# A block-causal attention and a two-layer feed-forward network on one core: one scheduling block with the detailed timing model, TensorE in program order

## The chip, the cores and the metric

The kernel runs on one core of a Trainium2 chip. The time is the device time of one execution in microseconds. Before the change it was 1272.79 us, the median of three runs (1271.26 to 1273.68).

## The reference

All arrays are float32.

```
scores = scale * matmul(q, k^T)              # batch 8, heads 8, 576 tokens, head size 64
mask   = block_i >= block_j                  # blocks of 64 tokens: a causal mask by blocks
attn   = softmax(where(mask, scores, -1e9))
x      = (attn @ v), heads side by side      # 4608 x 512
h      = x @ w_in                            # 4608 x 2048
g      = h where h >= 1, 0 where h <= -1, else (h + 1)^2 / 4
out    = g @ w_out                           # 4608 x 512
```

## The kernel before

A float32 operand that must keep its precision is split into a rounded high part and the rest, so that products run as two or three faster matmuls. The two weight matrices are split by `convert` in 64 pieces of 128x256. A piece is a load on the SP queue, two multiplications on ScalarE (L165, L166), three operations on VectorE (L167, L170, L173), then GpSimd (L179), ScalarE (L181) and GpSimd (L183). The pieces of `w_out` are gathered in `ws` tiles and written back to DRAM as `wo_split`.

Attention goes through 32 pairs of heads, pair 0 to pair 31, four for each batch. A pair is a generator of eight steps: loads and splits of q and k (`split_q`, `split_k`), their transposes on TensorE (`turned`, L346, and `turned_last`, L365), scores (`product`, L391 and L394), maximum on VectorE (L414), exponential on ScalarE with its sum read out (L418), normalisation (L400, L401, L424), transposes of the result (`turn`, L461 or L463; from pair 4 on the result first goes through a transfer, `as_float32r`), splits of it (L454, L456) and the product with v (L500). The next pair's transposes of q and k belong to the steps of the pair before it: the first transposes of its k, `nxt.turned(False, 0)`, stand at the end of the step that computes `cur.scores(1, 1)`. In the first two batches (pairs 0 to 7) the product with v is done in plain float32.

The network works on chunks of 512 tokens and 16 slices of 128 hidden units, 144 in all. `ffn_in` accumulates twelve matmuls in the one bank `ph` (L646), then ScalarE (L655), VectorE (L656, L659), ScalarE (L660) and GpSimd (L661) make `gh` and `gl`; `ffn_out` adds twelve matmuls into four banks `po` (L670, L675). From step 36 of attention on (the middle of pair 4) one network step, an `ffn_in` or an `ffn_out`, is emitted after each step of attention. What is left follows after the last pair.

The tiles of scores and transposes share PSUM banks, `work_bank`: three of them once the network runs. So a tile waits until what was in its bank three tiles earlier has been read.

What sets the order: the program emits instructions in the order above. A scheduler then orders each engine's queue by priority, the emission order, and by the readiness that a timing model gives, and also hands out the buffers. On the chip every queue is worked off strictly in its order. Before the change this is one simple timing model for all queues, TensorE's among them.

Of the kernel before, what the change touches and what calls it, by code (L numbers as in the profile page):

```python
# [23 lines left out]
def block_attn_then_ffn(  # L24
# [59 lines left out]


    ident_f = ffn.tile([P, 512], F32, tag="t", name="ident_f")[:, :P]
    make_identity(nc, ident_f)
    ident_r = const.tile([P, P], F32R, tag="ident", name="ident_r")
    nc.vector.tensor_copy(ident_r, ident_f)
    ident = ident_r.bitcast(F32)  # L90

    xh = const.tile([P, NCC, RING], F32R, tag="xh", name="xh")
    xl = const.tile([P, NCC, RING], F32R, tag="xl", name="xl")
    wih = const.tile([P, NCC, DF], F32R, tag="wih", name="wih")
    wil = const.tile([P, NCC, DF], F32R, tag="wil", name="wil")
    wo_split = dram.tile([NFC, P, 2, DM], F32, tag="wo_split", name="wo_split")
# [3 lines left out]
    qa = const.tile([P, 2, QW], F32R, tag="qa", name="qa")  # L100
    qb = const.tile([P, 2, QW], F32R, tag="qb", name="qb")
    ka = const.tile([P, 2, S], F32R, tag="ka", name="ka")
    kb = const.tile([P, 2, S], F32R, tag="kb", name="kb")

    def last_blocks(t_):

        view = t_[:, :, SM : SM + BLK]
        if t_.shape[2] == S:
            return view
        part, (_, two), cols = view.ap  # L110
        return bass.AP(tensor=view.tensor, offset=view.offset, ap=[part, [QW + BLK, two], cols])


    mrow = att1.tile([NTL, 2, S], F32R, tag="pb0", name="mrow")


    pcs = [const.tile([P, 2, BLK], F32R, tag=f"pcs{i}", name=f"pcs{i}") for i in range(2)]
    vsr = [const.tile([P, NTL + 1, 2, D], F32R, tag=f"vsr{j}", name=f"vsr{j}") for j in range(2)]

    mtmp = ffn.tile([P, 512], F32, tag="t", name="mtmp")  # L120
    msel = ffn.tile([P, 512], F32, tag="t", name="msel")
    nc.vector.memset(mtmp, 0.0)
    nc.vector.memset(msel[:NTL], 0.0)
    nc.gpsimd.affine_select(
        out=msel[:NTL, : NTL * BLK].rearrange("p (t c) -> p t c", c=BLK),
        in_=msel[:NTL, : NTL * BLK].rearrange("p (t c) -> p t c", c=BLK),
        compare_op=ALU.not_equal, fill=1.0, base=0,
        pattern=[[-1, NTL], [0, BLK]], channel_multiplier=1,
    )
    sel = msel[:NTL, : NTL * BLK].rearrange("p (t c) -> p t c", c=BLK)  # L130
    for side in range(2):
        nc.vector.tensor_copy(mrow[:, side, :512], mtmp[:NTL, :512])
        nc.vector.tensor_copy(mrow[:, side, 512:S], mtmp[:NTL, : S - 512])
    rows = mrow[:, :, :SM].rearrange("p s (t c) -> p s t c", c=P)
    nc.vector.tensor_copy(rows[:, 0, :, :BLK], sel)
    nc.vector.tensor_scalar_mul(rows[:, 1, :, BLK:], sel, MASKED)
    for t_ in (qa, qb):
        nc.vector.tensor_copy(
            t_[:, :, SM:], mtmp[:, : 2 * (QW - SM)].rearrange("p (h c) -> p h c", h=2)
        )  # L140
    for t_ in pcs:
        nc.vector.tensor_copy(t_[BLK:], mtmp[BLK:, : 2 * BLK].rearrange("p (h c) -> p h c", h=2))
    for t_ in vsr:
        nc.vector.tensor_copy(
            t_[BLK:, NTL, :, :], mtmp[BLK:, : 2 * D].rearrange("p (h c) -> p h c", h=2)
        )
    for j in range(2):
        nc.sync.dma_start(qa[D:KA, j, :S].bitcast(F32), mrow[:, 0, :].bitcast(F32))
        nc.sync.dma_start(ka[D:KA, j, :].bitcast(F32), mrow[:, 1, :].bitcast(F32))


    def convert(n, source, hi, lo, done):

        if n < BORROW and n % 2:
            bits = ffn.tile([P, CW, 2], I32, tag="t", name="bits")
            work = ffn.tile([P, 2, CW], F32, tag="gl", name="work")
        else:
            bits = conv.tile([P, CW, 2], I32, tag="bits", name="bits")
            work = conv2.tile([P, 2, CW], F32, tag="work", name="work")
        nc.sync.dma_start(bits, source.bitcast(I32).rearrange("p (n t) -> p n t", t=2))  # L160
        top, mag = work[:, 0, :], work[:, 1, :].bitcast(U32)
        low = bits[:, :, 0]


        nc.scalar.mul(top, bits[:, :, 1].bitcast(F32), 2.0**-112)  # L165
        nc.scalar.mul(low, low.bitcast(U32), 2.0**-29)  # L166
        nc.vector.tensor_scalar(  # L167
            out=top, in0=top, scalar1=F32_TOP, scalar2=-F32_TOP, op0=ALU.min, op1=ALU.max
        )
        nc.vector.tensor_scalar(  # L170
            out=mag, in0=top.bitcast(U32), scalar1=3, scalar2=None, op0=ALU.logical_shift_left
        )
        nc.vector.scalar_tensor_tensor(  # L173
            out=mag, in0=top.bitcast(U32), scalar=0x80000000, in1=mag,
            op0=ALU.bitwise_and, op1=ALU.bitwise_or,
        )
        yield
        w32 = mag.bitcast(I32)
        nc.gpsimd.tensor_tensor(out=w32, in0=w32, in1=low, op=ALU.add)  # L179
        w32 = w32.bitcast(F32)  # L180
        nc.scalar.copy(hi(), w32)  # L181
        yield
        nc.gpsimd.tensor_tensor(out=lo(), in0=w32, in1=hi().bitcast(F32), op=ALU.subtract)  # L183
        if done:
            done()

    def weight_pieces():

        for f0 in range(0, DF, CW):
            fs = slice(f0, f0 + CW)  # L190
            for cc in range(NCC):
                yield (
                    w_in[cc * P : (cc + 1) * P, fs],
                    lambda cc=cc, fs=fs: wih[:, cc, fs], lambda cc=cc, fs=fs: wil[:, cc, fs], None,
                )
            for fc in range(f0 // P, (f0 + CW) // P):
                ws = {}

                def part(w, d0, ws=ws):
                    if not ws:  # L200
                        ws[0] = ffn.tile([P, 2, DM], F32R, tag="wo", name="ws")
                    return ws[0][:, w, d0 : d0 + CW]

                for d0 in range(0, DM, CW):
                    yield (
                        w_out[fc * P : (fc + 1) * P, d0 : d0 + CW],
                        lambda p_=part, d0=d0: p_(0, d0), lambda p_=part, d0=d0: p_(1, d0),
                        None if d0 + CW < DM else
                        lambda fc=fc, ws=ws: nc.sync.dma_start(wo_split[fc], ws[0].bitcast(F32)),
                    )  # L210

    def prepare_weights():

        live = []
        for n, piece in enumerate(weight_pieces()):
            live = [c for c in live + [convert(n, *piece)] if next(c, True) is None]
            yield
        for _ in range(LAG):
            live = [c for c in live if next(c, True) is None]
            yield  # L220
# [3 lines left out]
    spare = {"n": 0, "of": []}  # L224

    def as_float32r(src, plain):

        if plain:
            if not spare["of"]:
                spare["of"] = [t_[:, :NTL, :, :].rearrange("p t h d -> p (t h d)") for t_ in vsr]  # L230
                spare["of"].append(att1.tile([P, S], F32R, tag="x32", name="prs")[:, :TCH])
                spare["end"] = att1.tile([P, G0 + P], F32R, tag="pa11", name="pre")[:, :BLK]
            moved = [spare["of"][spare["n"] % 3]]
            spare["n"] += 1
            if src.shape[1] > TCH:
                moved.append(spare["end"])
            for i, dst in enumerate(moved):
                n = min(TCH, src.shape[1] - i * TCH)
                nc.sync.dma_start(dst[:, :n].bitcast(F32), src[:, i * TCH : i * TCH + n])
            return moved  # L240
        moved = []
        for c0 in range(0, src.shape[1], TCH):
            n = min(TCH, src.shape[1] - c0)
            pool, tag = ((conv, "bits"), (conv2, "work"))[c0 > 0]
            dst = pool.tile([P, TCH], F32R, tag=tag, name="prr")
            nc.sync.dma_start(dst[:, :n].bitcast(F32), src[:, c0 : c0 + n])
            moved.append(dst)
        return moved


    class Pair:


        GROUPS = (((0, 0), (1, P)), ((2, 0),), ((3, 0),))

        def __init__(self, b, hp):
            self.b, self.hp = b, hp

            self.plain = b < PLAIN
            self.first = b == 0 and hp == 0  # L260

# [467 lines left out]
    for _ in ffn_steps:  # L729
        pass  # L730
# [30 lines left out]
```

## Time and profile before

| | us |
|---|---|
| median of three runs | 1272.79 |
| profiled execution, its own time | 1272.09 |
| its span, first to last instruction | 1270.3 |
| TensorE busy (matmuls) | 1210.7 |
| VectorE busy | 856.4 |
| ScalarE busy | 701.3 |
| GpSimd busy | 456.3 |
| mean granted TensorE clock | 0.985 |

The span is cut into stretches in the prediction, because its stages have different limits: the first 266 us hold pairs 0 to 7 and all conversions, the rest is a steady alternation of attention and network steps and, from about 1083 us, the network alone. In a row of the profile, "<-" behind a duration in brackets names what ended the engine's wait before that instruction, with the length of the idle time ahead of it. PE is TensorE, PEld its weight loads, DVE VectorE, ACT ScalarE, POOL GpSimd, SP the queue that issues the transfers.

### The profile page before, as it was taken

Reading aid. Unit: us, or ns where it says so; the run is one execution under the profiler, and the core shown is the slowest. Engines: PE = TensorE matmul, PEld = TensorE weight load, DVE = VectorE, ACT = ScalarE, POOL = GpSimd, SP = SyncE. Lnnn points to the kernel's source line nnn. Section 1 sums busy time; section 2 is a strip of 40 time slices with the busy share of each in tenths; the row PEclk is TensorE's granted clock in tenths of the full one; section 3 lists DMA queues with packets and bytes.
Section 4 is the critical chain, followed back from the end, with each engine's and each line's share of the span. In section 5 each row is a group of like instructions: output and inputs, shape, how many; then the busy total and the mean of one; then the engine's idle time right before and its main releaser. Section 6 shows DMA issues by size and latency. Waiting matters only on the chain.

```text
span 1270.3 us, 20591 instructions
## 1 busy us (share of the span) xinstructions
PE 1210.7 (95%) x6496; PEld 1018.4 (80%) x6496; DVE 856.4 (67%) x2164; ACT 701.3 (55%) x1827; POOL 456.3 (36%) x454
## 2 busy tenths in 40 slices
PE   5879887899999999999999999999999999999998
PEld 4667666688888888888888888888888888888886
DVE  8998877857776777777777777777777676222222
ACT  5877656546565655566556656555565564222222
POOL 3555655523332333333333333333333332222222
PEclk9888989899999999999999999999999999999999
DMA  5656666655444545564455545454445443322432
GB/s 157 182 165 213 196 228 210 212 184 173 148 152 147 191 144 161 158 193 149 148 162 168 178 141 161 153 181 143 152 154 184 151 132 117 127 92 97 133 100 100
DMA packets 146093, 201.30 MB, mean 158 GB/s; under 512 B 63152, under 2 KB 93872, under 8 KB 145984
## 3 DMA queue, kind: packets, MB, share of 16 engines
q1 hardware_dynamic: 145984, 199.98, 50.4%
q8 instruction: 52, 0.85, 0.3%
q14 instruction: 57, 0.47, 0.1%
HBM read 120.59 MB, written 17.83 MB: 109 GB/s over the span
## 4 chain that ended last, share of the span: by engine, by line
PE 68%; DVE 8%; ACT 4%; issue 3%; DMA 3%; POOL 2%; SPq 0%; ACTq 0%; POOLq 0%; DVEq 0%
PE ph L646 26%; PE po L670 16%; PE po L675 8%; PE ps_av L500 7%; PE ps_t L461 3%; PE ps_s L394 3%; PE ps_s L391 3%; ACT pr L418 2%; PE ps_qk L346 2%; DMA prr<-pr 2%; DVE t L656 2%; DVE nm L414 1%; DVE t L659 1%; DVE pr L424 1%; POOL work L179 1%
## 5 line engine op out<-in xcount | busy, mean ns | idle before, releaser
L661 POOL TENSOR_TENSOR gl<-t,gh 128x512 fp32r<-128x512 f32 x144 | 186.9, 1298 | 604.7 <-ACT gh L660 301.8
L670 PE MATMUL po<-wo,gh 128*128 128x512 f32 x1152 | 296.9, 399 | 0.1
L656 DVE SCALAR_TENSOR_TENSOR t<-t 128x512 f32<-128x512 f32 x144 | 112.9, 784 | 200.2 <-ACT t L655 198.5
L646 PE MATMUL ph<-xh,wih 128*128 128x512 f32 x576 | 237.6, 413 | 2.7 <-DVE t L659 1.8
L670 PEld LDWEIGHTS po<-wo,gh 128*128 128x128 f32 x1152 | 207.7, 188 | 39.3 <-ACT gh L660 0.6
L646 PE MATMUL ph<-xl,wih 128*128 128x512 f32 x576 | 227.4, 395 | 0.9 <-DVE xl L536 0.9
L646 PE MATMUL ph<-xh,wil 128*128 128x512 f32 x576 | 227.4, 395 | 0.0
L655 ACT ACTIVATE t<-ph 128x512 f32<-128x512 f32 x144 | 86.1, 598 | 184.7 <-PE ph L646 184.7
L418 ACT ACTIVATE pr<-ps_s,nm 128x128 f32<-128x128 f32 (+3 forms) x256 | 134.4, 529 | 50.6 <-DVE nm L414 50.3
L414 DVE TENSOR_REDUCE nm<-ps_s 128x1 f32<-128x128 f32 (+3 forms) x256 | 123.6, 485 | 48.7 <-PE ps_s L394 47.4
L675 PE MATMUL po<-wo,gl 128*128 128x512 f32 x576 | 155.3, 391 | 0.0
L660 ACT CAST gh<-t 128x512 fp32r<-128x512 f32 x144 | 89.6, 622 | 102.1 <-DVE t L659 101.7
L391 PE MATMUL ps_s<-ka,qa 68*128 68x288 f32 (+4 forms) x384 | 122.5, 334 | 9.1 <-ACT kb L351 4.2
L646 PEld LDWEIGHTS ph<-xh,wil 128*128 128x128 f32 x576 | 109.1, 189 | 24.1
L675 PEld LDWEIGHTS po<-wo,gl 128*128 128x128 f32 x576 | 108.1, 188 | 23.3
L646 PEld LDWEIGHTS ph<-xh,wih 128*128 128x128 f32 x576 | 109.1, 189 | 21.7 <-DVE t L659 2.4
L646 PEld LDWEIGHTS ph<-xl,wih 128*128 128x128 f32 x576 | 109.6, 190 | 20.2 <-DVE xl L536 1.5
L394 PE MATMUL ps_s<-kb,qb 128*128 128x288 f32 (+4 forms) x384 | 121.4, 323 | 0.0
L454 ACT CAST pb<-ps_t 128x512 fp32r<-128x512 f32 (+1 forms) x120 | 65.5, 546 | 85.6 <-PE ps_t L461 83.8
L424 DVE TENSOR_SCALAR pr<-pr,sm 128x128 f32<-128x128 f32 (+3 forms) x256 | 104.8, 430 | 4.0
L336 POOL TENSOR_TENSOR vsr<-vn,vsr 64x64 fp32r<-64x64 f32 (+1 forms) x96 | 72.8, 768 | 88.6 <-ACT vsr L335 88.6
L456 DVE TENSOR_TENSOR pb<-ps_t,pb 128x512 fp32r<-128x512 f32 (+1 forms) x120 | 75.6, 630 | 40.4 <-ACT pb L454 39.9
(101 smaller groups left out, 1961.4 us busy)
## 6 DMA issues: line engine op xcount, KB each, us to landing
wo<-wo_split SPq DMA_DIRECT2D x144, 512.0 KB, 3.4
prr<-pr SPq DMA_DIRECT2D x96, 192.0 KB, 2.7
prr<-pr SPq DMA_DIRECT2D x72, 256.0 KB, 2.6
out_dram<-ob SPq DMA_DIRECT2D x36, 256.0 KB, 3.9
qn<-in_q_dram SPq DMA_DIRECT2D x32, 256.0 KB, 2.9
kn<-in_k_dram SPq DMA_DIRECT2D x32, 256.0 KB, 2.9
bits<-in_moe_w_in_dram SPq DMA_DIRECT2D x32, 256.0 KB, 3.6
bits<-in_moe_w_out_dram SPq DMA_DIRECT2D x32, 256.0 KB, 3.2
```

The source lines that it names most:

```text
L391: nc.tensor.matmul(ps, qa[:KA, j, c0 : c0 + P], ka[:KA, j, k0 : k0 + n], start=first, stop=False)
L394: nc.tensor.matmul(ps, qb[:, j, c0 : c0 + P], kb[:, j, k0 : k0 + n], start=False, stop=last)
L414: nc.vector.tensor_reduce(out=nm[:, i : i + 1], in_=ps[:, cs], axis=AX.X, op=ALU.max, negate=True)
L418: nc.scalar.activation(pr[:, cs], ps[:, cs], AF.Exp, bias=nm[:, i : i + 1], scale=1.0, accum_out=sm[:, i : i + 1],)
L424: nc.vector.tensor_scalar_mul(pr[:, cs], pr[:, cs], sm[:, i : i + 1])
L500: nc.tensor.matmul(ps[:, lo_col:], vt, x, start=first and i == 0 and m == 0, stop=last and i == len(parts) - 1 and m == len(mov) - 1,)
L646: nc.tensor.matmul(ph, w[:, cc, fs], x[:, cc, xs], start=(cc == 0 and i == 0), stop=(cc == NCC - 1 and i == 2),)
L656: nc.vector.scalar_tensor_tensor(out=t_, in0=t_, scalar=1.0, in1=t_, op0=ALU.min, op1=ALU.mult)
L660: nc.scalar.copy(gh, t_)
L661: nc.gpsimd.tensor_tensor(out=gl, in0=t_, in1=gh.bitcast(F32), op=ALU.subtract)
L670: nc.tensor.matmul(po[tt], gh[:, ts_], wo[:, w, :], start=(fc == 0 and w == 0), stop=False)
L675: nc.tensor.matmul(po[tt], gl[:, ts_], wo[:, 0, :], start=False, stop=fc == NFC - 1)
```

## The change

One line is added after the definition of `work_bank`, and everything that follows in the function is indented under it. So each line below it has a number higher by one in the changed program.

```diff
+    with tc.block(schedule_with_timeline_sim=True), tc.manual_schedule(engines={mybir.EngineType.PE}):
...
-    ident_f = ffn.tile([P, 512], F32, tag="t", name="ident_f")[:, :P]
-    make_identity(nc, ident_f)
+        ident_f = ffn.tile([P, 512], F32, tag="t", name="ident_f")[:, :P]
+        make_identity(nc, ident_f)
...
```

TensorE's queue is now the emission order, instruction by instruction. The queues of VectorE, ScalarE, GpSimd and SP are ordered with the second, more detailed timing model, and the buffers are handed out along with that. No instruction is added or removed. From pair 8 on the queues differ in a few places for each pair; in the first eight pairs they differ throughout.

**TensorE, pair 14, the step of `cur.scores(1, 1)`.** `prr` is the transferred result of the softmax, `ks` the split k of pair 15, `ph` the network's bank. Before:

```order
L394 MATMUL ps_s<-kb,qb 128x384
L461 MATMUL ps_t<-ident_r,prr 128x128 x4
L461 MATMUL ps_t<-ident_r,prr 64x128
L646 MATMUL ph<-xh,wih 128x512
L646 MATMUL ph<-xl,wih 128x512
L646 MATMUL ph<-xh,wil 128x512
...
L346 MATMUL ps_qk<-ident_r,ks 128x128 x4
L646 MATMUL ph<-xh,wih 128x512
```

Changed:

```order
L395 MATMUL ps_s<-kb,qb 128x384
L462 MATMUL ps_t<-ident_r,prr 128x128 x4
L462 MATMUL ps_t<-ident_r,prr 64x128
L347 MATMUL ps_qk<-ident_r,ks 128x128 x4
L647 MATMUL ph<-xh,wih 128x512
L647 MATMUL ph<-xl,wih 128x512
```

The four transposes of k stood behind six of the step's twelve `ph` matmuls and now stand ahead of all of them. The place recurs in each pair from 8 to 30.

**ScalarE, the same step.** `gh` is the network's rounded slice, `pr,sm` an exponential with its sum, `pb` and `pcs` rounded parts of the turned result, `kb` the copy of the turned k. Before:

```order
L660 CAST gh<-t 128x512
L418 ACTIVATE pr,sm<-ps_s,nm 128x128
L418 ACTIVATE pr,sm<-ps_s,nm 128x256
L454 CAST pb_5432<-ps_t 128x4x2x64
L418 ACTIVATE pr,sm<-ps_s,nm 128x384
L454 CAST pcs_107<-ps_t 64x128
L351 CAST kb<-ps_qk 128x512
```

Changed:

```order
L419 ACTIVATE pr,sm<-ps_s,nm 128x128
L419 ACTIVATE pr,sm<-ps_s,nm 128x256
L661 CAST gh<-t 128x512
L455 CAST pb_5435<-ps_t 128x4x2x64
L455 CAST pcs_110<-ps_t 64x128
L419 ACTIVATE pr,sm<-ps_s,nm 128x384
L352 CAST kb<-ps_qk 128x512
```

The two exponentials of `cur.scores(1, 0)` move ahead of the `gh` cast, and the small cast of `pcs` moves ahead of the exponential of `cur.scores(1, 1)`. On VectorE the two reductions of `cur.scores(1, 0)` likewise move ahead of the network's L656.

**VectorE, the start of the program.** `ident_r` is the identity for the transposes, `qs` and `ks` the split q and k, `work` a weight conversion, `qa` and `ka` the copies of turned q and k. Before:

```order
L311 SCALAR_TENSOR_TENSOR qs<-qn,qs 128x9x64
L320 CAST ks<-kn 128x8x64
L320 CAST ks<-kn 128x64
L321 TENSOR_TENSOR ks<-kn,ks 128x9x64
L89 CAST ident_r<-ident_f 128x128
L135 CAST mrow<-msel 4x4x64
L136 TENSOR_SCALAR mrow<-msel 4x4x64
L167 TENSOR_SCALAR work<-work 128x256
L170 TENSOR_SCALAR work<-work 128x256
L353 CAST qa<-ps_qk 64x512
L353 CAST ka<-ps_qk 64x512
```

Changed:

```order
L90 CAST ident_r<-ident_f 128x128
...
L312 SCALAR_TENSOR_TENSOR qs<-qn,qs 128x9x64
L136 CAST mrow<-msel 4x4x64
L137 TENSOR_SCALAR mrow<-msel 4x4x64
L321 CAST ks<-kn 128x64
L322 TENSOR_TENSOR ks<-kn,ks 128x9x64
L354 CAST qa<-ps_qk 64x512
L354 CAST ka<-ps_qk 64x512
L415 TENSOR_REDUCE nm<-ps_s 128x1 x3
```

The identity's cast moves ahead of the splits, and the first weight conversion moves behind the copies `qa` and `ka` and the first reductions. ScalarE's queue moves its share of that conversion (L165) behind the copies of the turned q and k in the same way. After that the conversions run ahead: VectorE's queue holds 33 of the 64 ahead of the first reduction of pair 4, where it held 25.

More of the change, by code (lines that the diff above doesn't have):

```diff
@@ L114, in block_attn_then_ffn @@
[L114 to L129, printed above, removed]
@@ L141, in block_attn_then_ffn @@
[L141 to L185, printed above, removed]
@@ L212, in prepare_weights @@
[L212 to L248, printed above, removed]
@@ L496, in weighted @@
-        def weighted(self, ps, j, parts, first=True, last=True):
-            for i, (kt, lo_col, mov) in enumerate(parts):
-                vt = self.vs[j][: (BLK if self.plain and kt == NTL else P), kt, :, :]
-                for m, x in enumerate(mov):
-                    nc.tensor.matmul(
-                        ps[:, lo_col:], vt, x,
-                        start=first and i == 0 and m == 0,
-                        stop=last and i == len(parts) - 1 and m == len(mov) - 1,
-                    )
@@ L689, in feed_forward @@
-    def feed_forward():
-        prev = None
-        for c in range(NCH):
-            for fc in range(NFC):
-                cur = (c, fc, *ffn_in(c, fc))
-                yield
-                if prev is not None:
-                    if prev[1] == 0:
-                        po = [ps_o.tile([P, DM], F32, tag="po", name="po") for _ in range(NTT)]
-                    ffn_out(po, *prev)
-                    yield
-                prev = cur
-        ffn_out(po, *prev)
-        yield
-    START = 8 * NPAIR + 4
@@ new lines, in ffn_in @@
+        def ffn_in(c, fc):
+            at = (c * TCH) % RING
+            ph = ps_h.tile([P, 512], F32, tag="ph", name="ph")
+            fs = slice(fc * P, (fc + 1) * P)
+            xs = slice(at, at + TCH)
+            for cc in range(NCC):
+                for i, (w, x) in enumerate(((wih, xh), (wih, xl), (wil, xh))):
+                    nc.tensor.matmul(
+                        ph, w[:, cc, fs], x[:, cc, xs],
+                        start=(cc == 0 and i == 0), stop=(cc == NCC - 1 and i == 2),
+                    )
+            t_ = ffn.tile([P, TCH], F32, tag="t", name="t")
+            gh = ffn.tile([P, TCH], F32R, tag="gh", name="gh")
+            gl = ffn.tile([P, TCH], F32R, tag="gl", name="gl")
+            nc.scalar.activation(t_, ph, AF.Relu, bias=0.5, scale=0.5)
+            nc.vector.scalar_tensor_tensor(
+                out=t_, in0=t_, scalar=1.0, in1=t_, op0=ALU.min, op1=ALU.mult
+            )
+            nc.vector.tensor_tensor(out=t_, in0=ph, in1=t_, op=ALU.max)
+            nc.scalar.copy(gh, t_)
+            nc.gpsimd.tensor_tensor(out=gl, in0=t_, in1=gh.bitcast(F32), op=ALU.subtract)
+            wo = ffn.tile([P, 2, DM], F32R, tag="wo", name="wo")
+            nc.sync.dma_start(wo.bitcast(F32), wo_split[fc])
+            return gh, gl, wo
@@ new lines, in ffn_out @@
+        def ffn_out(po, c, fc, gh, gl, wo):
+            for tt in range(NTT):
+                ts_ = slice(tt * P, (tt + 1) * P)
+                for w in range(2):
+                    nc.tensor.matmul(
+                        po[tt], gh[:, ts_], wo[:, w, :], start=(fc == 0 and w == 0), stop=False
+                    )
+            for tt in range(NTT):
+                ts_ = slice(tt * P, (tt + 1) * P)
+                nc.tensor.matmul(po[tt], gl[:, ts_], wo[:, 0, :], start=False, stop=fc == NFC - 1)
+            if fc < NFC - 1:
+                return
+            for tt in range(NTT):
+                ob = conv.tile([P, DM], F32, tag="bits", name="ob") if tt % 2 else conv2.tile(
+                    [P, DM], F32, tag="work", name="ob"
+                )
+                if tt % 2:
+                    nc.scalar.copy(ob, po[tt])
+                else:
+                    nc.vector.tensor_copy(ob, po[tt])
+                r0 = c * TCH + tt * P
+                nc.sync.dma_start(out[r0 : r0 + P, :], ob)
@@ new lines, in feed_forward @@
+        def feed_forward():
+            prev = None
+            for c in range(NCH):
+                for fc in range(NFC):
+                    cur = (c, fc, *ffn_in(c, fc))
+                    yield
+                    if prev is not None:
+                        if prev[1] == 0:
+                            po = [ps_o.tile([P, DM], F32, tag="po", name="po") for _ in range(NTT)]
+                        ffn_out(po, *prev)
+                        yield
+                    prev = cur
+            ffn_out(po, *prev)
+            yield
```

933 lines of the change are left out of this document (491 added, 442 removed).

## The prediction

> **What bounds the kernel now.** I read the page's span and busy shares first, then the busy time by stretches, then the waits, then the order of time at one place.
>
> ```profile
> span 1270.3 us, 20591 instructions
> PE 1210.7 (95%) x6496; PEld 1018.4 (80%) x6496; DVE 856.4 (67%) x2164; ACT 701.3 (55%) x1827; POOL 456.3 (36%) x454
> ```
> TensorE is busy for 95% of the span, so only about 60 us can be won anywhere. Where they lie is shown by stretches: up to the first scores, pairs 0 to 3, pairs 4 to 7, pairs 8 to 31 and the end. Pair 4 starts at 100.56 and pair 8 at 265.95, each with its first reduction of scores.
>
> ```profile
> 0.00:14.00 14.00, 3.81 (x23) 3.62 (x24) 9.12 (x29) 4.50 (x10) 2.52 (x10) 1.00 0.52 132
> 14.00:100.60 86.60, 70.65 (x366) 57.28 (x366) 79.83 (x246) 69.04 (x211) 46.67 (x57) 0.88 0.60 177
> 100.60:266.00 165.40, 144.66 (x713) 113.84 (x712) 129.46 (x323) 104.49 (x297) 91.59 (x109) 0.95 0.67 214
> 266.00:1083.00 817.00, 809.35 (x4602) 693.85 (x4601) 588.57 (x1498) 479.37 (x1240) 271.44 (x244) 1.00 0.51 157
> 1083.00:1271.00 188.00, 182.19 (x800) 149.82 (x798) 49.40 (x72) 43.87 (x73) 44.09 (x34) 1.00 0.32 107
> ...
> 477.00:510.65 33.65, 33.42 (x193) 28.71 (x193) 24.61 (x64) 19.83 (x51) 11.50 (x10) 1.00 0.48 152
> ```
> After the length come busy PE, PEld, DVE, ACT and POOL, then the granted clock. In pairs 0 to 3 VectorE is the bound: 79.83 of 86.60 us. In pairs 4 to 7 nothing is saturated: TensorE 144.66 of 165.40 us at a clock of 0.95, VectorE 129.46. From 266 us on TensorE works without a break (809.35 of 817.00), so there each microsecond in which its queue stands still is added to the end. The last row is one period of that stretch, 33.65 us for a pair.
>
> **The change, part by part.** 1. TensorE's queue in pairs 8 to 31. It was nearly the program's order already. Of the places that differ one recurs in each of pairs 8 to 30, 23 times: the four transposes of the next pair's k stood behind the first 6 (17 places) or 7 (6 places) of the twelve `ph` matmuls of that step, and now stand ahead of them. Here is that place in pair 14, TensorE first, then VectorE and ScalarE.
>
> ```profile
> 491.28 0.35 PE L391 MATMUL ps_s<-ka,qa 68*128 68x384 f32 x1
> 491.47 0.34 PE L394 MATMUL ps_s<-kb,qb 128*128 128x384 f32 x1
> 491.65 0.53 PE L461 MATMUL ps_t<-ident_r,prr 128*128 128x128 f32 x5
> 492.01 0.45 PE L646 MATMUL ph<-xh,wih 128*128 128x512 f32 x1
> 492.30 0.40 PE L646 MATMUL ph<-xl,wih 128*128 128x512 f32 x1
> ...
> 493.22 0.39 PE L646 MATMUL ph<-xh,wil 128*128 128x512 f32 x1
> 493.83 0.54 PE L346 MATMUL ps_qk<-ident_r,ks 128*128 128x128 f32 x4 [0.23 <-ACT pr L418]
> 494.21 0.46 PE L646 MATMUL ph<-xh,wih 128*128 128x512 f32 x1
> ```
> ```profile
> 491.22 0.60 DVE L400 TENSOR_SCALAR sm<-sm 128x2 f32<-128x2 f32 x1 [0.57 <-ACT pr L418]
> ...
> 492.52 0.55 DVE L414 TENSOR_REDUCE nm<-ps_s 128x1 f32<-128x384 f32 x1
> ```
> ```profile
> 492.15 0.59 ACT L454 CAST pb<-ps_t 128x512 fp32r<-128x512 f32 x1 [0.96 <-PE ps_t L461]
> 493.11 0.58 ACT L418 ACTIVATE pr<-ps_s,nm 128x384 f32<-128x384 f32 x1 [0.37 <-DVE nm L414]
> 493.59 0.19 ACT L418 ACTIVATION_READ_ACCUMULATOR pr<-ps_s,nm 128x1 f32 x1
> 493.68 0.25 ACT L454 CAST pcs<-ps_t 64x128 fp32r<-64x128 f32 x1
> ```
> The transposes write the bank that held this step's scores. They wait for reduction and exponential of them, released at 493.78, and start at 493.83. The chain is the same in the changed program; what goes is its cover, six matmuls from 492.01 to 493.45. The queue reaches the transposes at 492.01 and stands, and everything behind them stands too: the twelve `ph` matmuls, then all of `ffn_out`. The cover is 17 x 6 + 6 x 7 = 144 matmuls of 0.23 us (492.30 to 493.22 is four of them), 33.1 us. Two things come off. In the new queues the casts of `pb` and `pcs` stand ahead of the exponential and the reduction is earlier (the two reductions and exponentials of the step before move ahead of the `t` and `gh` work), so the exponential starts when the casts end, 492.74 plus about 0.23, near 492.97 in place of 493.11: 0.14 us, 3.2 us in 23 places. And the waits quoted below name 13 stops at these transposes, so in some 8 places TensorE came after the release, by up to one matmul, 0.2 us: 1.6 us. **Sum +28 us.** From below: the reduction cannot start before the scores end (491.81), and reduction, exponential and read-out take 0.55 + 0.58 + 0.10 with two hand-overs of 0.05, release near 493.1; TensorE then loses 1.1 - 0.38 = 0.7 us, 16 us in all. From above: no link shorter and the cast of `pcs` (0.25) on the chain, 33.1 + 5.8 = 39 us. I take 28, which is what the row at 492.15 gives.
>
> The other moves in these pairs are a few places on VectorE and ScalarE. Here and there a normalisation whose result is transferred before its turn comes later by a few short instructions of the q and k split. That costs nothing while the transfers have margin, and the waits show they have:
>
> ```profile
> PE ps_qk L346 <- ACT pr L418: 2.9, 13, 0.3
> PE ps_t L461 <- DMA prr<-pr: 1.6, 4, 0.6
> PE ps_t L461 <- ACT pr L418: 0.8, 2, 0.5
> ```
> These are all of TensorE's named waits from 266 to 1050 us: 5.3 us. It is also the most that this part could win.
>
> 2. The start.
>
> ```profile
> 7.57 0.56 PEld L346 LDWEIGHTS ps_qk<-ident_r,qs 128*128 128x128 f32 x4 [7.57 <-DVE ident_r L89]
> 10.26 0.43 ACT L165 ACTIVATE work<-bits 128x256 f32<-128x256 f32 x1 [8.25 <-DMA bits<-in_moe_w_in_dram]
> 10.72 0.29 DVE L167 TENSOR_SCALAR work<-work 128x256 f32<-128x256 f32 x1 [2.81 <-ACT work L165]
> 12.72 0.47 PE L391 MATMUL ps_s<-ka,qa 68*128 68x128 f32 x1 [2.62 <-DVE ka L353]
> ```
> A weight conversion stands ahead of the first `qb` and `qa` copies and holds both queues until its data land. Now the conversions stand behind, and the identity's cast ahead of the q and k splits. That wins the 2.81 us, and I take **-3 us** (bounds -5 and 0).
>
> 3. The conversions. Counting VectorE's rows ahead of the first reduction of pair 4, 25 of the 64 conversions stood there and now 33; ahead of pair 8 it is all 64 in both.
>
> ```profile
> L167 DVE TENSOR_SCALAR work<-work 128x256 f32<-128x256 f32 x24 | 11.3, 476 | 0.8 <-ACT work L165 0.8
> L173 DVE SCALAR_TENSOR_TENSOR work<-work 128x256 uint32<-128x256 uint32 x24 | 10.9, 453 | 0.1
> L170 DVE TENSOR_SCALAR work<-work 128x256 uint32<-128x256 uint32 x24 | 10.1, 424 | 0.1
> ```
> One costs 476 + 453 + 424 = 1353 ns, so 8 more on the saturated engine put pair 4 **+10.8 us** later (bounds +4, if they fit into the 6.8 us that VectorE is idle there, and +14). Pairs 4 to 7 get 8 fewer. Against that stands TensorE's fixed order there: some fifteen places where attention's matmuls stood behind `ph` or `po` matmuls now stand ahead of them. The first bounds are 0 and the 20.7 us that TensorE idles in these pairs, and since VectorE is only 78% busy I take -6. The second costs between 0 and 15 x 1.4 = 21 us by the steady place; many of those waits are there already, so I take +10. The twelve matmuls of the first `ffn_in`, which filled gaps of pairs 2 to 4, now run in pair 4: 12 x 0.23, **+2.8 us**. Sum of parts 2 and 3: -3 + 10.8 - 6 + 10 + 2.8 = +14.6. The last two gains and losses overlap in time, since a later pair 4 meets queues that are emptier, so I take **+10**, and -15 to +25 as bounds.
>
> **The clock at the new stops.** It is halved in some stretches of the first 266 us, in windows of 3.41 us. Three such windows, each with the one that follows:
>
> ```profile
> 177.73:181.14 3.41, 1.36 (x6) 0.84 (x6) 3.38 (x6) 1.87 (x6) 3.41 (x5) 1.00 0.91 290
> 181.14:184.56 3.42, 3.15 (x6) 2.17 (x7) 3.42 (x9) 1.35 (x6) 2.70 (x3) 0.50 0.17 55
> 198.21:201.62 3.41, 1.88 (x14) 1.53 (x13) 1.59 (x6) 2.44 (x7) 2.10 (x3) 1.00 0.62 184
> 201.62:205.04 3.42, 3.12 (x16) 2.11 (x14) 3.01 (x7) 2.68 (x9) 0.99 (x1) 1.00 0.56 161
> ```
> With 2.05 us idle in a window the next one is halved, with 1.53 us it is not. The new stop leaves 493.69 - 492.18 = 1.5 us idle, on the safe side by little. I take no cost, and the other case is a rival. The Trainium skill, page "TensorE: Matmul & The Clock Gate", section "Part 1: The HAM clock gate", says that the clock is halved after an idle window of about 3.4 us, counted in windows that run freely. By that rule no stop here costs clock and the sum stays as it is; the trace agrees on the window's length, 3.41 us, and not on the condition, since a window with 1.36 us of work was followed by a halved one.
>
> **Sum.** The profiled execution took 1272.09 us by its own time (span 1270.3 and 1.8 around it), 0.7 below the median 1272.79. 1272.1 + 28 + 10 = **1310 us**.
>
> **Rivals.**
> - Halved clock: at half of the 23 stops the clock drops for one window. Half of 3.42 us is lost, 1.7 us x 12 = 20 us: 1330 us. For it: the margin of 0.3 us above. Against: the stretch 198.21.
> - A jammed first quarter: the early conversions and the fixed order cost their upper bounds, +25 in place of +10: 1325 us. For it: VectorE at 92%. Against: pairs 4 to 7 have slack.
> - A half-price stop: the chain shortens to its lower bound (16 us) and the first quarter is neutral: 1288 us.
> - Faster: pairs 4 to 7, freed of 8 conversions, run at TensorE's own pace. The 20.7 us of idle and the 0.05 x 165.4 = 8.3 us of missing clock go, the start wins 3, the earlier conversions cost only 4, and the stops cost their lower bound: 1272.1 - 20.7 - 8.3 - 3 + 4 + 2.8 + 16 = 1263 us. It decides once the first quarter wins more than the stops cost, 16 to 28 us. Against: VectorE's total work up to 266 us is unchanged.
> - The new order does nothing measurable: the transposes' release comes before TensorE reaches them, so that no stop arises, and the early parts cancel, 1272 us. Against: scores end at 491.81 and the transposes are reached at 492.01.
>
> **How the numbers follow.** Forecast 0.58, halved clock 0.13, jammed quarter 0.11, half price 0.10, faster 0.05, no change 0.03. The range 1286 to 1334 takes in the first four. About 0.2%, 2.5 us, is what a measurement of this kernel can tell from no change: faster 0.05, within it 0.03, slower 0.92.
>
> **What would show it.** Waits of TensorE at the k transposes for the exponential, 23 of about 1.5 us, some 34 us in place of 2.9; a pair's period after pair 8 of 33.65 + 1.2 = 34.9 us; first scores near 12.72 - 3 = 9.7 us; pair 4 starting at 105 to 115 us; the clock at 1.00 after pair 8. If those waits are absent, part 1 is wrong; if pair 8 starts before 255 us or after 295 us, parts 2 and 3 are.

## The result, and the profile after

The changed kernel takes 1368.19 us (median of 4 runs, 1364.06 to 1373.63), the kernel before 1272.59 us beside it: a ratio of 1.0754, with a 95% interval of 1.0715 to 1.0794. It is slower, as forecast, but by 95.6 us where 37.4 were forecast. The profiled execution took 1373.63 us, the longest of the four, so that the terms below add up to a little more than 95.6.

The page's first lines, and the busy time by stretches cut at the same events as before (first scores, pair 4, pair 8; columns as in the prediction):

```profile
span 1371.9 us, 20596 instructions
...
PE 1237.4 (90%) x6496; PEld 1042.1 (76%) x6496; DVE 890.1 (65%) x2164; ACT 705.4 (51%) x1827; POOL 445.4 (32%) x454
```
```profile
0.00:11.40 11.40, 3.29 (x19) 2.92 (x19) 7.60 (x24) 2.96 (x4) 1.85 (x9) 1.00 0.29 81
11.40:120.85 109.45, 76.14 (x362) 61.84 (x361) 99.39 (x276) 79.36 (x243) 58.45 (x74) 0.83 0.60 182
120.85:283.70 162.85, 143.08 (x715) 114.94 (x714) 122.48 (x296) 96.37 (x267) 80.34 (x93) 0.96 0.61 195
283.70:1182.00 898.30, 830.16 (x4594) 710.24 (x4593) 610.81 (x1497) 481.94 (x1240) 259.42 (x243) 0.98 0.48 143
```

Pair 8 starts at 283.7 us in place of 265.9: 17.8 us are lost up to there. From pair 8 to the end it takes 1371.9 - 283.7 = 1088.2 us, where it took 1270.3 - 265.9 = 1004.4: 83.8 us more. In this part TensorE was hardly idle before (7.7 of 817 us); now it misses 68 of 898 us. The waits of TensorE from 300 to 1150 us (us in total, times, longest) say where:

```profile
PE ps_t L462 <- DMA prr<-pr: 32.8, 21, 2.4
PE ps_qk L347 <- ACT pr L419: 22.8, 17, 1.3
PE ps_qk L347 <- DVE pb L457: 9.2, 6, 1.6
PE ps_t L462 <- DVE t L657: 3.1, 2, 1.6
```

The second and third row are one place, the k transposes of the prediction: 23 stops, 32.0 us together; the trace puts 17 of them down to the exponential and six to the split of `pb` on VectorE. The first and the fourth are a second place that the prediction does not have: the transposes of the softmax result, `turn(0, 2)`, which wait for its transfer: one stop in each pair from 9 to 29, and two short waits elsewhere. (At the two stops of the fourth row, too, the transfer lands about 0.1 us before they start.) Both places in pair 11, in order of time, each wait in brackets:

```profile
410.10 0.48 SPq L301 DMA_DIRECT2D kn<-in_k_dram  x1
410.67 0.53 SPq L664 DMA_DIRECT2D wo<-wo_split  x1
...
411.06 0.38 PE L462 MATMUL ps_t<-ident_r,prr 128*128 128x128 f32 x3
411.15 0.48 DVE L425 TENSOR_SCALAR pr<-pr,sm 128x512 f32<-128x512 f32 x1
411.67 0.50 SPq L247 DMA_DIRECT2D prr<-pr  x1
...
416.07 0.51 PE L462 MATMUL ps_t<-ident_r,prr 128*128 128x128 f32 x4 [1.35 <-DMA prr<-pr]
...
421.85 0.54 PE L347 MATMUL ps_qk<-ident_r,ks 128*128 128x128 f32 x4 [1.34 <-ACT pr L419]
```

Before, pair 14, the same instructions:

```profile
484.30 0.38 PE L461 MATMUL ps_t<-ident_r,prr 128*128 128x128 f32 x3
...
484.55 0.54 SPq L246 DMA_DIRECT2D prr<-pr  x1
...
485.19 0.54 SPq L663 DMA_DIRECT2D wo<-wo_split  x1
...
487.80 0.47 PE L461 MATMUL ps_t<-ident_r,prr 128*128 128x128 f32 x4
```

The two transfers have changed places on SP: the network's `wo` load of 512 KB now goes out one microsecond ahead of the 256 KB of `prr`. How long a transfer takes from issue to landing, first all transfers of this line between 300 and 1050 us before, also those of 192 KB, then the one of 411.67 after:

```profile
DMA to landing us min/median/max: 1.9/2.6/4.2
```
```profile
DMA to landing us min/median/max: 4.3/4.3/4.3
```

In pairs 9 to 29 the trace gives, from issue to the completion of this one transfer, 2.3 to 3.5 us before (median 2.8) and 4.0 to 5.4 us in the changed kernel (median 4.7). In pairs 8 and 30 both kernels send the load ahead, without a stop at the transposes. But in pair 31 the kernel before does so too, and it has the stop:

```profile
1055.66 0.33 SPq L663 DMA_DIRECT2D wo<-wo_split  x1
1056.65 4.71 SPq L246 DMA_DIRECT2D prr<-pr  x3
```
```profile
1061.80 0.50 PE L461 MATMUL ps_t<-ident_r,prr 128*128 128x128 f32 x4 [1.59 <-DMA prr<-pr]
```

The list of waits that the prediction quotes ends at 1050 us and so leaves this one out.

Lastly the clock. A window of 3.41 us with such a stop, and the next one:

```profile
451.00:454.41 3.41, 1.49 (x12) 1.39 (x13) 1.93 (x5) 1.12 (x3) 0.00 (x0) 1.00 0.41 145
454.41:457.83 3.42, 3.42 (x10) 2.68 (x9) 1.84 (x5) 1.56 (x6) 1.27 (x1) 0.50 0.19 43
```

Behind pair 8 the changed kernel has 13 windows at half clock, 44.4 us, where the kernel before has none (both without the last microseconds of the program). Half of that is lost, 22 us; TensorE's busy time in the rows says the same, 830.16 us for 4594 matmuls against 809.35 us for 4602, 21 us more.

### The profile page after: what moved, and what is told of

The parts are those of the page before. It is cut to its first block, busy times and chain, and to the rows that moved or that the text cites. A ratio compares the mean times of both kernels' runs of the same rounds, so it can differ in the third digit from the quotient of the medians.

```text
span 1371.9 us, 20596 instructions
## 1 busy us (share of the span) xinstructions
PE 1237.4 (90%) x6496; PEld 1042.1 (76%) x6496; DVE 890.1 (65%) x2164; ACT 705.4 (51%) x1827; POOL 445.4 (32%) x454
## 3 DMA queue, kind: packets, MB, share of 16 engines
q1 hardware_dynamic: 145984, 199.98, 47.8%
## 4 chain that ended last, share of the span: by engine, by line
PE 66%; DVE 17%; DMA 10%; ACT 3%; issue 2%; SPq 1%; POOL 0%; ACTq 0%; DVEq 0%; POOLq 0%
PE ph L647 23%; PE po L671 17%; PE po L676 8%; PE ps_av L501 7%; DMA prr<-pr 7%; PE ps_t L462 3%; PE ps_qk L347 3%; DVE t L657 3%; PE ps_s L392 2%; PE ps_s L395 2%; DVE pr L425 2%; DVE nm L415 2%; DVE work L168 2%; DVE work L174 2%; DVE work L171 1%
## 5 line engine op out<-in xcount | busy, mean ns | idle before, releaser
L662 POOL TENSOR_TENSOR gl<-t,gh 128x512 fp32r<-128x512 f32 x144 | 190.6, 1323 | 551.2 <-ACT gh L661 347.0
L671 PE MATMUL po<-wo,gh 128*128 128x512 f32 x1152 | 311.9, 415 | 0.1
L671 PEld LDWEIGHTS po<-wo,gh 128*128 128x128 f32 x1152 | 218.1, 197 | 42.9 <-ACT gh L661 0.6
L415 DVE TENSOR_REDUCE nm<-ps_s 128x1 f32<-128x128 f32 (+3 forms) x256 | 118.8, 484 | 167.5 <-PE ps_s L395 166.9
L657 DVE SCALAR_TENSOR_TENSOR t<-t 128x512 f32<-128x512 f32 x144 | 126.2, 876 | 132.2 <-ACT t L656 131.3
L656 ACT ACTIVATE t<-ph 128x512 f32<-128x512 f32 x144 | 86.1, 598 | 219.6 <-PE ph L647 218.9
L676 PE MATMUL po<-wo,gl 128*128 128x512 f32 x576 | 158.2, 397 | 0.0
L425 DVE TENSOR_SCALAR pr<-pr,sm 128x128 f32<-128x128 f32 (+3 forms) x256 | 130.3, 529 | 4.8
L676 PEld LDWEIGHTS po<-wo,gl 128*128 128x128 f32 x576 | 111.5, 194 | 24.7
L337 POOL TENSOR_TENSOR vsr<-vn,vsr 64x64 fp32r<-64x64 f32 (+1 forms) x96 | 53.7, 569 | 219.4 <-ACT vsr L336 219.4
```

What stands on the lines that cost most here:

```text
L415: nc.vector.tensor_reduce(out=nm[:, i : i + 1], in_=ps[:, cs], axis=AX.X, op=ALU.max, negate=True)
L425: nc.vector.tensor_scalar_mul(pr[:, cs], pr[:, cs], sm[:, i : i + 1])
L657: nc.vector.scalar_tensor_tensor(out=t_, in0=t_, scalar=1.0, in1=t_, op0=ALU.min, op1=ALU.mult)
L662: nc.gpsimd.tensor_tensor(out=gl, in0=t_, in1=gh.bitcast(F32), op=ALU.subtract)
L671: nc.tensor.matmul(po[tt], gh[:, ts_], wo[:, w, :], start=(fc == 0 and w == 0), stop=False)
L676: nc.tensor.matmul(po[tt], gl[:, ts_], wo[:, 0, :], start=False, stop=fc == NFC - 1)
```

## The experiments

Theory A: behind pair 8 the loss is two stops in each pair, at the k transposes (from TensorE's emission order) and at `turn(0, 2)` (from the detailed model's order on SP), and the half clock that they bring. Theory B gives most of the loss to one part of the change alone. C and D, E and F concern the first 266 us and stand with their runs. The runs at a glance; stops and half clock are counted behind pair 8, "period" is the mean of pairs 9 to 29, and the kernel before took 1269.8 to 1271.4 us beside them (medians). e1 to e7 and e11 are single executions; repeated ones of the changed kernel lay up to 10 us apart. For e8, e9 and e10 "us" is the median of several executions, and the other columns are read from one of them:

| run | us | pair 4 | pair 8 | period | k stops | transfer stops | half clock |
|---|---|---|---|---|---|---|---|
| before | 1272.1 | 100.6 | 265.9 | 33.70 | 3.2 | 4.4 | 0 |
| after | 1373.6 | 120.9 | 283.7 | 37.62 | 32.0 | 36.0 | 44.4 |
| e1 | 1329.9 | 108.4 | 284.0 | 35.49 | 35.5 | 4.2 | 17.1 |
| e2 | 1347.3 | 121.6 | 285.2 | 36.35 | 0.4 | 37.1 | 47.8 |
| e3 | 1321.2 | 122.0 | 284.2 | 35.00 | 33.7 | 0.4 | 10.2 |
| e4 | 1289.2 | 122.0 | 285.5 | 33.64 | 2.1 | 2.2 | 0 |
| e5 | 1304.4 | 107.0 | 303.2 | 33.53 | 3.1 | 0.7 | 0 |
| e6 | 1287.9 | 109.1 | 285.7 | 33.58 | 2.7 | 1.0 | 0 |
| e7 | 1447.9 | 117.8 | 286.6 | 40.87 | 75.4 at many places together | | 228.7 |
| e8 | 1277.8 | 101.8 | 271.0 | 33.73 | 3.6 | 2.7 | 0 |
| e9 | 1318.5 | 102.1 | 268.9 | 35.62 | 36.2 | 1.8 | 23.9 |
| e10 | 1272.1 | 101.3 | 267.8 | 33.72 | 3.7 | 2.2 | 0 |
| e11 | 1334.1 | 99.3 | 266.3 | 36.74 | 0.3 | 46.1 | 51.2 |

**e1: TensorE's order alone**, with the simple model for the other queues.

```diff
-    with tc.block(schedule_with_timeline_sim=True), tc.manual_schedule(engines={mybir.EngineType.PE}):
+    with tc.block(), tc.manual_schedule(engines={mybir.EngineType.PE}):
```

> TensorE in program order, all other queues with the simple timing model. Theory A (three costs from pair 8 on: the stop at the k transposes, about 30 us, comes of the fixed order; the stop at the turn of the scores' last group, about 34 us, comes of the detailed model, which puts the wo load ahead of that group's transfer on SP; the halved clock, about 24 us, comes of the second stop): the first stop alone, waits of TensorE for the exponential at the k transposes of about 30 us, for transfers under 5 us, no halved window after pair 8, first eight pairs within 10 us of before: about 1305 us. Theory B (all of it comes of the fixed order, which leaves TensorE no other work at any wait): both stops and the halved windows are there, 1350 to 1370 us.

Waits of TensorE from 300 to 1050 us:

```profile
PE ps_qk L347 <- ACT pr L419: 32.2, 21, 2.0
PE ps_t L462 <- DMA prr<-pr: 2.8, 6, 1.4
```

The k stops are all there, the transfer stops are not: the first come from TensorE's order, the second come with the detailed model. Two things A did not have: five halved windows, and 18 us lost before pair 8. So the time missed A's number too.

**e2: the k transposes behind six `ph` matmuls again.** In pairs 8 to 30 `nxt.turned(False, 0)` is emitted within the next `ffn_in`.

```diff
-                    nxt.turned(False, 0)
+                    if nxt.b >= PLAIN and cur.b >= PLAIN:
+                        inside.append(lambda nxt=nxt: nxt.turned(False, 0))
+                    else:
+                        nxt.turned(False, 0)
...
             for cc in range(NCC):
+                if cc == NCC // 2 and inside:
+                    inside.pop()()
```

> The changed kernel with the next pair's first k transposes emitted in the middle of the step's twelve ph matmuls, in pairs 8 to 30. Theory A: the wait for the exponential goes from about 30 us to about 3, the wait for transfers stays at about 33 us and most of the halved windows with it: 1368 less 30, about 1338 us. Theory B: TensorE waits for the chain elsewhere, so little is won, above 1355 us.

```profile
PE ps_t L462 <- DMA prr<-pr: 26.6, 19, 2.8
PE ps_t L462 <- DVE t L664: 7.4, 5, 1.7
```

The k stops are gone, and with them 26.4 us of the span. The transfer stops stay, and so does the half clock (14 windows, 47.8 us). The time is 9 us above A's.

**e3: the `wo` load behind the transfer**, in the one step of each pair in which it stood ahead; `moves` holds the 256 KB transfers.

```diff
...
-            nc.sync.dma_start(wo.bitcast(F32), wo_split[fc])
+            with tc.issue_after(moves[-1]) if moves and now["step"] % 8 == 3 else ExitStack():
+                nc.sync.dma_start(wo.bitcast(F32), wo_split[fc])
```

> The changed kernel with the wo load of the fourth step of a pair queued on SP behind the transfer of the softmax result of the scores' last group. Theory A: that transfer lands in about 2.8 us in place of 4.3, the wait for transfers goes from 33 us to under 8, and the halved windows after pair 8 go with it, since a stop of 1.34 us alone leaves less idle time in a window than every halved one had: 1368 less 27 less 24, about 1315 us. Theory B (the order on SP does not matter): 1360 to 1370 us. If the clock falls at the k transposes too, 1325 to 1340 us.

```profile
PE ps_qk L350 <- ACT pr L422: 21.4, 16, 1.3
PE ps_qk L350 <- DVE pb L460: 10.9, 6, 2.2
```

The transfer stops go from 36.0 to 0.4 us with this one pair of issues turned round, and of 13 halved windows 3 are left: 52.8 us of the span. The transfer lands after 2.3 to 2.9 us again (pairs 9 to 29). The time, 1321.2 us, lies between A's 1315 and the 1325 that was named for a clock that also falls at the k transposes, which it does three times.

**e4: both edits.**

> The changed kernel with both edits. Theory A: pairs 8 to 31 run as before the change, 33.7 us each, the clock stays at 1.00 there, and what remains is the later start of pair 8, about 18 us: 1285 to 1292 us. Theory B: above 1340 us.

```profile
285.50:1100.00 814.50, 810.19 (x4610) 694.97 (x4610) 609.27 (x1498) 484.07 (x1242) 260.68 (x244) 1.00 0.52 158
```

Behind pair 8 TensorE works without a break again, at full clock, and this part takes 1287.1 - 285.5 = 1001.6 us, as before the change (1004.4). So the 83.8 us are these two stops and their clock, and within a few microseconds nothing else. What remains is lost before pair 8.

**e5 and e6: the conversions kept back.** On top of e4, either their loads on SP (e5) or their first operation on VectorE (e6) keep the program's order, so that fewer of them run ahead of pair 4: 20 and 22, where the changed kernel has 33.

```diff
-            nc.sync.dma_start(bits, source.bitcast(I32).rearrange("p (n t) -> p n t", t=2))
+            tc.keep_in_program_order(
+                nc.sync.dma_start(bits, source.bitcast(I32).rearrange("p (n t) -> p n t", t=2))
+            )
...
-            nc.vector.tensor_scalar(
+            tc.keep_in_program_order(nc.vector.tensor_scalar(
...
```

> The kernel of e4 with the loads of the weight conversions kept in program order on SP, so that 20 conversions in place of 33 stand ahead of pair 4's first reduction. Theory C (the later start of pair 4, 121 us in place of 101, comes of the conversions that run ahead of attention's work on VectorE): pair 4 starts near 103 us, pair 8 near 270 to 275 us since the conversions left come in pairs 4 to 7, 1273 to 1279 us in all. Theory D (all 64 conversions have to be done by pair 8, so their order does not matter): pair 8 at 282 to 287 us as in e4, 1285 to 1290 us.

> The kernel of e4 with each conversion's first VectorE operation kept in program order on VectorE, the loads left free: 22 conversions stand ahead of pair 4's first reduction, and no normalisation stands behind a conversion that was emitted after it. Theory C: pair 4 near 103 us, 1273 to 1279 us. Theory D: 1285 to 1290 us.

Pair 4 comes 13 to 15 us earlier, at 107.0 and 109.1 us, but pairs 4 to 7 then take 196.2 and 176.6 us where e4 takes 163.5. Nothing is won (e6), or 15 us are lost (e5). The conversions held back burden pairs 4 to 7 instead, so their place alone is not the cause of the early loss. Theory C is refuted. e6 comes out as theory D has it (pair 8 at 285.7 us), e5 as neither (303.2); why e5 loses more was not followed.

**e7: the detailed model alone**, for TensorE's queue as well.

```diff
-    with tc.block(schedule_with_timeline_sim=True), tc.manual_schedule(engines={mybir.EngineType.PE}):
+    with tc.block(schedule_with_timeline_sim=True):
```

> The detailed model for all queues, TensorE's too. In this order TensorE holds the wo loads ahead of the transfers as in the changed kernel, but may put other matmuls where the k transposes and turns would stop. Theory A: no stop at the k transposes, the transfers land late but are partly covered, 1290 to 1330 us with pair 4 near 121 us. If the detailed model is what costs everything, 1360 us or more.

Busy time from pair 8 on, and within it two windows:

```profile
286.60:1250.00 963.40, 892.33 (x4559) 745.79 (x4559) 601.77 (x1488) 472.66 (x1231) 258.40 (x243) 0.89 0.43 133
```
```profile
758.60:762.10 3.50, 2.35 (x12) 1.59 (x10) 2.56 (x9) 1.99 (x6) 0.00 (x0) 0.50 0.00 0
762.10:765.50 3.40, 0.84 (x7) 0.87 (x8) 1.67 (x7) 0.75 (x3) 0.00 (x0) 0.50 0.64 207
```

The idle time in this stretch, 963.4 - 892.3 = 71 us, is hardly longer than in the changed kernel (68), but it is scattered over a dozen places, and the halved stretches join up, the longest to 44 us: 228.7 us at half clock. So the 1290 to 1330 us of theory A, which had no clock in it, were missed by far. TensorE's program order does not cause the loss of the whole; against the model alone it saves 74 us of the span.

**e8: the new start alone**, on the kernel before: the identity's cast ahead of the split of q, that ahead of the split of k, and the first conversion kept in program order.

```diff
+        if n == 0:
+            tc.keep_in_program_order(first)
...
-        first.split_q()
-        first.split_k()
+        with tc.issue_after(cast.ins):
+            first.split_q()
+        with tc.issue_after(first.last_q.ins):
+            first.split_k()
```

> The kernel before the change with only its start put in the changed kernel's order: the identity's cast ahead of the q split, the q split ahead of the k split, the first conversion behind the copies of the turned q and k on ScalarE. The first reduction comes at about 11.4 us in place of 14.0. If that carries through, 2.6 us less than before, 1269.5 to 1270 us; if VectorE's work up to pair 4 sets the pace whatever the start, no difference.

Slower by half a per cent, a ratio of 1.0055 (1.0035 to 1.0075): the first reduction comes at 13.4 us, not at 11.4, and pair 8 at 271.0. The edit did not bring the start of the changed kernel, and up to pair 8 it put the other queues in another order too, so it says nothing of that start's worth. What costs the 5 us later was not followed.

**e9: TensorE in program order from pair 8 on**, on the kernel before; up to there the queues stand as before.

```diff
+    late = ExitStack()
     for i, _ in enumerate(attention_steps()):
+        if i == 64:
+            late.enter_context(tc.manual_schedule(engines={mybir.EngineType.PE}))
```

> The kernel before, with TensorE held to the emission order only from pair 8 on; up to there every queue stands as before, and the simple timing model orders the others. Theory E (the early loss comes from TensorE's fixed order in pairs 0 to 7, and the late loss from its order after them, and the two are independent): pair 8 starts at 266 us, within 2 us of before; behind it the stops at the k transposes come back, about 35 us in 23 places, the transfer waits stay near 3 us, and the whole is 1270 + 40 = 1310 us, where 40 us is what the same order cost behind pair 8 in the run with TensorE's order alone (1328.0 - 284.0 against 1270.3 - 265.9). Rival F (the early loss has another source, and the order alone does not bring it): pair 8 at 284 us, the whole near 1328.

```profile
PE ps_qk L346 <- ACT pr L418: 33.1, 21, 1.7
PE ps_t L461 <- DMA prr<-pr: 1.7, 4, 0.6
```

Ratio 1.0373 (1.0356 to 1.0391), 1318.5 us: above E's 1310, as seven windows are halved. Pair 8 starts at 268.9 us, 2.9 us later than before where E allowed 2, but not at 284 as in e1, so the early loss of e1 comes from the fixed order in pairs 0 to 7, together with the other queues, which the scheduler orders differently there once TensorE's is fixed. In e9, e10 and e11 the operations of all five queues up to pair 8 stand in the order of before, and pair 8 starts at 268.9, 267.8 and 266.3 us against 265.9: by 3 us this start varies without any change of order.

**e10: the same with e2's edit.**

> As the run with TensorE's order from pair 8 on, and in pairs 8 to 30 the k transposes emitted behind six of the ph matmuls; a few other queues differ early by some places. Theory E: the k stops go to under 3 us, pair 8 starts at 264 to 270 us, nothing is left of the loss, 1266 to 1274 us. Rival F: the fixed order costs something besides the stops, a period of 33.9 us or more and at least 5 us in all, 1278 us or more.

```profile
267.80:1083.00 815.20, 809.36 (x4601) 693.53 (x4600) 588.07 (x1498) 479.27 (x1240) 271.18 (x244) 1.00 0.51 157
```

Ratio 1.0003 (0.9993 to 1.0013): the fixed order costs nothing behind pair 8 once the k transposes are emitted with their cover. It brings nothing either: no version here beats the kernel before.

**e11: the load ahead, in the kernel before.** Simple model, TensorE's order free; the load of `wo` is emitted early and the transfer kept behind it.

```diff
-            nc.sync.dma_start(dst[:, :n].bitcast(F32), src[:, c0 : c0 + n])
+            with tc.issue_after(last["load"]) if early else ExitStack():
+                nc.sync.dma_start(dst[:, :n].bitcast(F32), src[:, c0 : c0 + n])
...
+            if cur.b >= PLAIN:
+                early.append(load_wo(last["fc"]))
             cur.scores(0, 2)
...
```

> The kernel before, simple model and free order of TensorE, with one thing added: in pairs 8 to 31 the 512 KB load of wo is put ahead of the transfer of scores(0,2) on SP. The early queues differ in some places too, so it is read from pair 8 on. Theory (the load ahead is enough to make the transfer late): the transfer's landing goes from 2.6 to 4 us or more, TensorE's waits for it from 3.4 to 25-33 us, the period from 33.70 to 34.7-35.1 us, the time to 1295-1310 us. Rival (the stop needs the later normalisation of the changed queues as well, or TensorE's free order covers it): the waits stay under 10 us and the period under 34.1.

SP's two issues and the stop in one pair:

```profile
495.99 0.53 SPq L646 DMA_DIRECT2D wo<-wo_split  x1
496.62 0.50 SPq L249 DMA_DIRECT2D prr<-pr  x1
...
501.40 0.51 PE L464 MATMUL ps_t<-ident_r,prr 128*128 128x128 f32 x4 [1.91 <-DMA prr<-pr]
```

The load ahead is enough by itself: 46.1 us of stops and 15 halved windows, 51.2 us. The transfer lands after 3.9 to 5.5 us (pairs 9 to 29, median 4.7). The theory's 25 to 33 us were too low, and it had no clock in it.

## Why the direction was right and the size wrong

By the two spans 101.6 us were lost. The terms, in the prediction's order:

- **The k transposes: +28 forecast, +28.8 measured** (32.0 against 3.2 us). The place, the count of 23, the lost cover and, at 17 of the 23, the chain through the exponential were right; e2 removes it for 26.4 us. (23 less 13 named stops are 10 places and not 8, as the prediction has it, which changes its sum by 0.4 us.)
- **"That costs nothing while the transfers have margin": 0 forecast, +31.6 measured** (36.0 against 4.4 us). This is the step that failed. The waits it quoted showed that TensorE hardly waited for transfers, and that was taken for a margin that would stay. But the margin was small, and it hung on SP's order. Before, in pair 14, 484.55 plus the median landing of 2.6 gives 487.15, and the transposes came at 487.80: 0.65 us. In the changed kernel, in pair 11, the transfer is issued 0.61 us behind the three transposes in place of 0.25, and lands after 4.27 us in place of 2.6: together 2.03 us later. 2.03 - 0.65 = 1.38 us, and the row says 1.35. Four fifths of it is the load ahead; e3 and e11 show it by undoing it and by doing it alone. Of the moves behind pair 8 the prediction names those on VectorE and ScalarE and leaves out SP's, on which the two transfers changed places; what else is in flight when a transfer starts is no term of its sum. How the load delays the transfer on its way no row shows. The Trainium skill, page "DMA: Bandwidth & Descriptors", section "Two DMAs through the same engine are not ordered", says that within one queue of one DMA engine descriptors start in order. No row here shows the starts; the landings came in the order of issue, the load of 410.67 at 415.1 (4.4 us) and the transfer behind it at 415.9.
- **The clock: 0 forecast, 22 measured**, half of 44.4 us. The forecast called a stop of 1.5 us safe "by little", from two windows of the kernel before. A third window of that kernel already said otherwise: with 1.33 us idle it was followed by a halved one.

```profile
157.25:160.66 3.41, 2.08 (x14) 1.50 (x14) 3.27 (x9) 2.82 (x10) 2.63 (x3) 1.00 0.76 252
160.66:164.07 3.41, 3.41 (x9) 2.64 (x9) 2.83 (x9) 2.07 (x6) 1.50 (x3) 0.50 0.61 198
```

The k stops alone halve 5 windows (e1) and 7 (e9). The transfer stops, which it did not have, halve most: e3 without them leaves 3, e2 with them alone has 14. That the rival's 20 us came out is luck: it counted half of the k stops.

- **The first eight pairs: +10 forecast, +17.8 measured**, within the bounds of -15 to +25. The start is right (-3; first scores at 10.11 in place of 12.72). The count of 33 conversions is right, but pair 4 comes 20.3 us later, outside the 105 to 115 us named. The term that was too small is the conversions' 10.8 us (bounds 4 to 14). Between the first scores and pair 4 ten more stand in the changed kernel and not eight, since the one that stood ahead of the first scores has moved in too, and each takes 1444 ns in place of 1353:

```profile
L168 DVE TENSOR_SCALAR work<-work 128x256 f32<-128x256 f32 x34 | 18.0, 528 | 2.3 <-ACT work L166 2.3
L174 DVE SCALAR_TENSOR_TENSOR work<-work 128x256 uint32<-128x256 uint32 x33 | 16.3, 502 | 0.2
L171 DVE TENSOR_SCALAR work<-work 128x256 uint32<-128x256 uint32 x34 | 13.9, 414 | 0.2
```

That is 48.2 us where it was 32.3, so 15.9 us more; VectorE is busy for 99.39 of the 109.45 us of this stretch, 19.6 us more than before. On TensorE it shows as waits for normalisations that stand behind conversions on VectorE, until pair 4, first after, then before:

```profile
PE ps_t L464 <- DVE pr L425: 23.1, 12, 6.1
```
```profile
PE ps_t L463 <- DVE sm L400: 7.4, 3, 3.8
PE ps_t L463 <- DVE pr L424: 2.2, 4, 0.9
```

Pairs 4 to 7 then take 162.85 in place of 165.4 us, 2.5 us less, where 6.8 more were forecast. So pair 4 comes 12.5 us later than the terms gave (-3 + 10.8), pairs 4 to 7 are 9.3 us shorter, and that their sum of 14.6, taken as 10 in the forecast, lies near the 17.8 measured is luck.

28.8 + 31.6 + 22.2 + 17.8 = 100.4 us, of the 101.6. The range failed because no rival had a late transfer, and because two cases that stood side by side as rivals, the clock and the first quarter, both came about on top of the forecast.

**Still open:** how the early loss comes about in detail. TensorE's fixed order alone brings 15 to 18 us of it (e1 against e9 and against before) and the detailed model alone 20.7 (e7), by different ways: with the first, pairs 4 to 7 take 175.6 us, with the second pair 4 comes at 117.8. Together they do not add up, and holding conversions back only moves the loss (e5, e6).

## What to carry to other kernels

A wait that is short in the profile is no margin: subtract a transfer's landing from its first use, and when a queue's order changes, read off for each transfer with a small difference what is now in flight ahead of it. When TensorE's queue is to follow the program, the program must be written with the cover in it, as e10 does. And where TensorE is the bound, price a repeated stop with the clock: each halved window cost 1.7 us more here, and in the changed kernel 44 stops brought 13 of them.

## What the runs showed of the hardware

The clock follows windows of 3.41 us, and a window need not be idle to be followed by a halved one. Over the six runs with stops of one or two microseconds (after, e1, e2, e3, e9, e11), all windows behind pair 8 that ran at full clock, by TensorE's idle time within the window:

| idle in the window, us | windows | next one halved |
|---|---|---|
| under 1.2 | 1666 | 0 |
| 1.2 to 1.4 | 46 | 1 |
| 1.4 to 1.5 | 10 | 2 |
| 1.5 to 1.6 | 14 | 7 |
| 1.6 to 1.7 | 21 | 15 |
| 1.7 to 1.8 | 6 | 5 |
| 1.8 and more | 26 | 26 |

In these runs the point lies near 1.55 us, somewhat under half of the window. It is no sharp threshold, and idle time alone does not decide: in e7, whose idle time is scattered, behind pair 8 all nine windows with 1.2 to 1.6 us were followed by a halved one, and one with 0.99 us. In all 13 traces, from start to end, no full-clock window with under 0.8 us idle was followed by a halved one, and each of the 103 with 1.8 us or more was. The windows lie on one grid from start to end of a trace, so a stop can be cut by the edge of a window; that may be why 23 k stops halved 5 windows once and 7 another time, but it was not tested. The other surprise is the price of an order on one queue: 512 KB issued 0.5 to 1.6 us ahead brought the landing of a 256 KB transfer from a median of 2.8 us to 4.7 (pairs 9 to 29).
